# A two-layer block with attention and a mixture of experts: the first expert's last rows are listed on chip, roots for two blocks at once, shorter groups of products

## The chip, the cores and the metric

The kernel runs on one core of one Trainium2 chip. TensorE (PE) multiplies matrices out of on-chip memory (SBUF) into eight accumulation banks (PSUM); VectorE (DVE), ScalarE (ACT) and GpSimd (POOL) work on rows of 128 partitions; SyncE (SP) issues DMA transfers, and GpSimd issues the indirect ones, which gather or scatter rows by a list of row numbers. Each engine runs its own instructions strictly in order and waits on semaphores for the others. The metric is device time in microseconds, lower is better.

## The reference

```
h  = x + attention(layernorm(x))          # 2048 tokens x 512, 32 heads of 16, window 256, causal
g  = softmax(layernorm(h) @ wg)           # 8 experts; the two best, their weights scaled to sum 1
out = h + sum over the 2 experts of  w * (gelu(layernorm(h) @ w1[e]) @ w2[e])    # w1: 512x1376, w2: 1376x512
```

All is float32. The kernel writes each large product as three products of rounded halves: high x high, high x low, low x high.

## The kernel before

**Stages.** The tokens go through in four chunks of 512 (`NC` = 4). For each chunk come layernorm and the projections, attention by groups of four heads, and `project(c)`: output projection, residual, second layernorm, gate, and the choice of two experts (`route`). After that `experts()` goes through the eight experts, one after the other. Expert 0 comes first always; the other seven come by size, for which `rank_experts` sorts the counts (`run`) and SyncE reads the order (`pick_expert`).

**The table.** For each choice of a token, `route` computes a slot number: expert times `SLOTS` plus the place among that expert's tokens. On GpSimd, `scatter` writes the token's row number and its weight (8 bytes) into that slot of `table` in DRAM. An expert's rows are then found by `fetch` (SyncE: a piece of the table into `tb_t`), `turn_x` (GpSimd: an indirect gather of 128 rows of the normalized tokens `xnd` into `xg_t`; TensorE: four transposes; ScalarE and VectorE: the high and low halves), `up` (w1, then gelu), `down` (w2), a scaling by the weight, and an indirect scatter-add into the output.

**The first expert's two parts.** Expert 0 holds 598 slots: five tiles of 128 columns, the last of 86. Its first 384 slots (`EARLY`) are filled by chunks 0 to 2, so their fetch, their gathers and their up-projections (384 columns) run beside the last chunk's projection and routing. For that, the last chunk's counts for expert 0 are raised to 384 at least. The other two tiles (214 columns) need the last chunk: its last scatter, then a second fetch (`f1`), then two gathers.

**The last chunk** (`end`) is routed in two halves of two blocks of 128 tokens: for each half `s1` (two largest gates, VectorE), `s3` (TensorE: places by a triangular 0/1 matrix), `s2`, `s2b` (weights), `s4` (slots), then four scatters. `rstd` computes the inverse root of the variance on GpSimd, for one block at a time here, and the normalized block goes to `xnd` by DMA and through a transpose (`turn`) to the gate's product.

**What sets the order.** Every piece of work is a task with an engine, an estimated duration, a priority and buffers. `Plan.order` runs through all tasks in estimated time and writes out one fixed order; an engine takes the ready task of the lowest priority. Dependencies given to `plan.after` or in a task's list shape only this order; on the chip an instruction waits for the data that it uses. Two raw-weight buffers (`m_raw`), two temporaries and seven PSUM banks (`one`) are handed out in that order too.

The prediction's steps touch: L1316 and L1321 (gather and transposes of `turn_x`), L1348 (`up`), L1380 (`down`), L1243 (`fetch`), L1102 (scatter), L1209 (load of w1), L480 (low halves on GpSimd), L476 (high halves on ScalarE), L998 and L1005 (transposes and products of the gate), L1266 (small products for the later experts), L1092 to L1098 (`s4`), and L1134 (the first step of the sort).

## Time and profile before

| | us |
|---|---|
| runs shown | 1045.19, 1047.86, 1051.26 |
| median | 1047.86 |
| profiled execution: its own time | 1044.5 |
| profiled execution: span of the trace | 1042.4 |

The profile is of one execution. Its times count from the first instruction. Busy shares of the span are 98% for TensorE, 62% for VectorE, 52% for ScalarE and 60% for GpSimd. The last chunk's projection and routing, with expert 0's early part among them, lie between some 480 and 550 us, and the experts fill the time from there to the end. In a timeline, each row gives the start, the duration from the first start to the last end of the merged instructions, the engine, the line, what is written and read with its shape, and the count; in square brackets the idle time before it and what ended it. A float32 product shows as two instructions. Rows of the granted clock give TensorE's clock as a share of 2.4 GHz.

### The profile page before, as it was taken

The numbers are of one execution on the slowest core, as the hardware profiler recorded it, in microseconds if no ns is written. First come the engines' busy times: TensorE is split into PE (matmuls) and PEld (weight loads), VectorE is DVE, ScalarE is ACT, GpSimd is POOL, SyncE is SP. The second block draws the span as 40 slices with busy tenths as digits, with TensorE's granted clock in tenths as the row PEclk, the third lists the DMA queues.
The fourth block names the chain that finished last, engine by engine and source line by source line (L and its number), as shares of the span: only waits on it lengthen the run. The fifth ranks groups of instructions, "written<-read, shape, count | busy, mean of one in ns | idle before, by whom it ended". The sixth has DMA issues, their size and how long they took to land. (4 is left out here: it accounts for less than half of the span.)

```text
span 1042.4 us, 19919 instructions
## 1 busy us (share of the span) xinstructions
PE 1016.8 (98%) x6722; PEld 842.0 (81%) x6722; DVE 645.6 (62%) x1951; ACT 536.9 (52%) x1143; POOL 623.3 (60%) x986
## 2 busy tenths in 40 slices
PE   8999999999999999998898999999999999999997
PEld 5877777877777777754887898998999989878795
DVE  8888876887677777787752556345453554544440
ACT  3487747575766656577631555163462543525340
POOL 5687749777887958758495144186483763834111
PEclk9999999999999999999998999999999999999999
DMA  6999877768696978764516344264444544454522
GB/s 214 291 249 240 250 190 214 224 179 202 191 251 164 200 159 210 201 167 110 190 49 148 97 141 113 63 153 111 115 97 128 157 94 105 123 139 151 124 77 29
DMA packets 143887, 164.48 MB, mean 158 GB/s; under 512 B 68587, under 2 KB 86571, under 8 KB 143776
## 3 DMA queue, kind: packets, MB, share of 16 engines
q1 hardware_dynamic: 128448, 145.96, 50.3%
q0 software_dynamic: 15328, 17.16, 9.9%
q8 instruction: 55, 0.90, 0.4%
q14 instruction: 56, 0.46, 0.2%
HBM read 111.10 MB, written 51.43 MB: 156 GB/s over the span
## 5 line engine op out<-in xcount | busy, mean ns | idle before, releaser
L735 DVE CUSTOM_DVE_ANT_0 one<-one,masked 128x320 f32<-128x320 f32 (+4 forms) x512 | 230.3, 494 | 57.9 <-PE one L730 55.0
L1348 PE MATMUL one<-mr 128*128 128x288 f32 (+14 forms) x1716 | 255.9, 310 | 1.3 <-ACT mr L476 0.7
L1348 PEld LDWEIGHTS one<-mr 128*128 128x128 f32 (+1 forms) x1716 | 244.5, 187 | 10.1 <-ACT mr L476 0.9
L785 ACT ACTIVATE zone<-one 128x384 f32<-128x384 f32 (+1 forms) x480 | 208.6, 495 | 80.1 <-PE one L779 60.6
L811 POOL TENSOR_SCALAR_AFFINE_SELECT zone<-zone 128x256 f32<-128x256 f32 (+1 forms) x332 | 151.1, 479 | 61.2 <-ACT zone L785 59.4
L1380 PE MATMUL one<-zone,mr 128*128 128x512 f32 (+4 forms) x648 | 154.9, 394 | 0.0
L480 POOL TENSOR_TENSOR mr<-mf,mr 128x512 fp32r<-128x512 f32 (+4 forms) x99 | 123.8, 1262 | 41.7 <-ACT mr L476 39.9
L1380 PEld LDWEIGHTS one<-zone,mr 128*128 128x128 f32 (+4 forms) x648 | 117.0, 182 | 31.4
L779 PE MATMUL one<-mr 98*128 98x384 f32 (+1 forms) x592 | 138.5, 327 | 3.1 <-ACT zone L785 1.9
L476 ACT CAST mr<-mf 128x512 fp32r<-128x512 f32 (+6 forms) x152 | 108.3, 734 | 46.0 <-DMA mf<-in_A_wqk_dram 15.3
L779 PEld LDWEIGHTS one<-mr 98*128 98x128 f32 x592 | 96.0, 190 | 42.9 <-ACT zone L785 14.1
L730 PE MATMUL one<-mr 96*128 96x320 f32 (+4 forms) x512 | 122.8, 315 | 1.5 <-DVE mx L735 0.9
L1287 POOL DMA_INDIRECT mf<-xnd,mf x94 | 106.4, 1132 | 28.8 <-issue 26.9
L1403 POOL DMA_INDIRECT out_dram<-mf,tb x24 | 41.5, 1730 | 130.6 <-DVE mf L1391 116.4
L478 DVE TENSOR_TENSOR mr<-one,mr 128x512 fp32r<-128x512 f32 (+16 forms) x161 | 79.1, 509 | 58.3 <-ACT mr L476 58.0
L1362 ACT ACTIVATE one<-one 128x288 f32<-128x288 f32 (+13 forms) x132 | 54.7, 415 | 104.1 <-PE one L1348 103.2
L661 PE MATMUL one<-mr 128*128 128x512 f32 (+1 forms) x396 | 103.7, 389 | 3.0 <-ACT mr L476 2.8
L730 PEld LDWEIGHTS one<-mr 96*128 96x128 f32 x512 | 87.7, 190 | 22.2 <-DVE mx L735 11.6
L1403 POOL DMA_INDIRECT out_dram<-mf x40 | 65.9, 1648 | 65.6 <-DVE mf L1433 57.1
L835 PE MATMUL oT<-zone 128*17 128x384 f32 (+2 forms) x1408 | 95.7, 389 | 0.1
L476 ACT CAST mr<-one 128x512 fp32r<-128x512 f32 (+16 forms) x161 | 70.6, 448 | 31.5 <-PE one L1321 17.3
L476 ACT CAST zone<-mf 128x512 fp32r<-128x512 f32 x72 | 42.1, 620 | 78.0 <-PE one L1423 48.5
(189 smaller groups left out, 1282.9 us busy)
## 6 DMA issues: line engine op xcount, KB each, us to landing
mf<-in_B_w_dram SPq DMA_DIRECT2D x32, 688.0 KB
mf<-in_B_w_dram SPq DMA_DIRECT2D x40, 512.0 KB
qkd<-mr SPq DMA_DIRECT2D x29, 512.0 KB
mr<-qkd SPq DMA_DIRECT2D x128, 96.0 KB
mr<-qkd SPq DMA_DIRECT2D x32, 384.0 KB
mf<-in_A_x_dram SPq DMA_DIRECT2D x32, 256.0 KB
mf<-in_A_wqk_dram SPq DMA_DIRECT2D x32, 256.0 KB
qkd<-mr SPq DMA_DIRECT2D x64, 128.0 KB
```

The lines of the kernel that those rows point to most:

```text
L476: a = add("ACT", 51 + n * 0.86, lambda: nc.scalar.copy(dst_h(), src()), deps, prio, bufs)
L480: b = add("POOL", 60 + n * 2.3, lambda: nc.gpsimd.tensor_sub(dst_l(), src(), f32(dst_h())), [a], prio, bufs)
L661: nc.tensor.matmul(single[bk.h][:, s], wt()[:, int(i == 1), k * 128:(k + 1) * 128], xt[:, k, s], start=(i == 0 and k == 0), stop=(i == 2 a ...
L730: nc.tensor.matmul(view()[:, j], q_of(slot)[0:96, h + j, b].rearrange("p e q -> p (e q)"), K[slot.h][0:96, h + j, (b + k0) * 64:(b + 5) * ...
L735: nc.vector.tensor_tensor_reduce(v, v, masked[:, 320 - n:], scale=1.0, scalar=NEG, op0=OP.add, op1=OP.max, accum_out=mx_t[slot.h][:, h + j ...
L779: nc.tensor.matmul(single[bk.h][:, off:off + w], K[slot.h][0:98, h // 2, r * 128:(r + 1) * 128], q_of(slot)[0:98, h // 2, 2 * b:2 * b + 2 ...
L785: return add("ACT", 51 + n * 0.833, lambda: nc.scalar.activation(dst(), single[bk.h][:, 0:n].rearrange(order, **({"e": 2, "q": 64} if "e" ...
L811: nc.gpsimd.affine_select(v, v, pattern=[[0, v.shape[1]], [-1 if far else 1, 128]], compare_op=OP.is_gt if far else OP.is_ge, fill=0.0, ba ...
L1287: nc.gpsimd.indirect_dma_start(out=xg_t[i][:, t * 128:(t + 1) * 128], out_offset=None, in_=xnd4, in_offset=bass.IndirectOffsetOnAxis(ap=ql ...
L1348: nc.tensor.matmul(bank(), a[:, k, f * 128:f * 128 + w], spot[b][:, k, c0:c1], start=(i == 0), stop=(i == 11))
L1380: nc.tensor.matmul(single[bk.h][:n], h[a][:w], spot["w2"][2 * f + b][:w], start=(f == 0 and q == 0), stop=(f == NF - 1 and q == 2))
L1403: d = nc.gpsimd.indirect_dma_start(in_offset=None, compute_op=OP.add, **kw)
```

## The change

**On-chip list.** Expert 0's piece of the table is fetched once, all five tiles, before any scatter of the last chunk (`plan.after` holds those back behind the fetch). What the last chunk adds is then found by products: `numbers` puts the slot numbers 385 to 640 into a row (`late_no`), `find` compares it with each token's slot in expert 0 (`late_v`) and so gets a 0/1 matrix of 128 tokens by 256 slots for each block, and `pick_late` multiplies that matrix with two columns, token number and weight (`late_r`), summed over the four blocks in one bank. `merge` takes the larger of the fetched and the picked token number, adds the weights, and writes both into `tb_t`. The two late gathers follow from that. The scatters of the last chunk stay, since the overflow path of expert 0 and the other experts read the table.

**Roots** for two blocks at once in the last chunk (`rstd` with n = 2), with the two blocks' normalizations after them; two buffers for the transposed block (`nt_2`).

**Shorter groups.** Expert 0's `up` is three tasks of four products, its `down` one task for each 128 rows of w2. Expert 0's low halves of w2 all go to VectorE.

The sort now stands after `merge`. The core of the diff (`...` marks what is left out):

```diff
-                f0 = fetch(0, b + -12, sum((route_done[c] for c in range(NC - 1)), []) + [xn_done[i] for i in range(4 * NC - 4)], 0, EARLY // 128)
-                f1 = fetch(0, b - 8, all_routes + all_xn, EARLY // 128, nt)
+                f0 = fetch(0, F0_PRIO, sum((route_done[c] for c in range(NC - 1)), []) + [xn_done[i] for i in range(4 * NC - 4)], 0, nt)
+                for t in route_done[NC - 1]:
+                    plan.after(t, [f0])
+                tb0 = tb_t[0][:, EARLY // 128:nt]
+                old = add("DVE", 100, lambda: nc.vector.tensor_copy(late_t, tb0[:, :, 0]), [f0] + hot[:1], b - 10)
+                def merge():
+                    ps = single[hot[1].h][:, 0:4].rearrange("p (i q) -> p i q", q=2)
+                    nc.vector.tensor_tensor(late_t, late_t, ps[:, :, 0], op=OP.max)
+                    nc.vector.tensor_copy(tb0[:, :, 0], late_t)
+                    nc.vector.tensor_add(tb0.bitcast(F32)[:, :, 1], tb0.bitcast(F32)[:, :, 1], ps[:, :, 1])
+                f1 = add("DVE", 550, merge, [old] + hot[2:], 36, [hot[1]])
+                xg_use[2] = p2_free + hot[2:]
+                plan.after(sort, [f1])
...
+            def numbers():
+                nc.gpsimd.iota(late_no.bitcast(I32), pattern=[[1, 256]], base=EARLY + 1, channel_multiplier=0)
+            def number_rows():
+                nc.vector.tensor_copy(late_no, late_no.bitcast(I32))
+                nc.vector.tensor_copy(late_r[:, :, 0], tok[:, 4 * c:4 * c + 4])
...
+                for i in range(2):
+                    Vv.tensor_mul((late_r[:, b0:b0 + nb, 1], late_w[:, 0:nb])[i], oh[:, i, :, 0], w[:, i, :, 1])
+                Vv.tensor_add(late_r[:, b0:b0 + nb, 1], late_r[:, b0:b0 + nb, 1], late_w[:, 0:nb])
...
+        def find():
+            pos = single[bk.h][:, 0:nb * E].rearrange("p (b e) -> p b e", e=E)
+            Vv.tensor_add(t["u"], pos, over(e_pos))
+            Vv.scalar_tensor_tensor(late_v[:, b0:b0 + nb], t["u"][:, :, 0], 1.0, t["m"][:, :, 0], op0=OP.add, op1=OP.mult)
+            for b in range(nb):
+                Vv.tensor_scalar(late_p[b], late_no, late_v[:, b0 + b:b0 + b + 1], None, op0=OP.is_equal)
+        def pick_late():
+            ps = single[hot[1].h][:, 0:4].rearrange("p (i q) -> p i q", q=2)
+            for b in range(nb):
+                for i in range(2):
+                    nc.tensor.matmul(ps[:, i], late_p[b][:, i * 128:(i + 1) * 128], late_r[:, b0 + b], start=(b0 + b + i == 0), stop=(b0 + b == 3),
...
+                    root = rstd(lambda b0=b0: mv_t[0][:, b0:b0 + 2, 1], lambda b0=b0: ry_t[0][:, b0:b0 + 2], seen[-2:], pb + 0.4, 2)
...
-                                 src, dd, lo="POOL" if e == 0 and f >= 3 else "DVE"))
+                                 src, dd))
...
-            for f0, f1 in ((0, 4), (4, 8), (8, 10), (10, NF)):
+            for f0, f1 in [(f, f + 1) for f in range(NF)] if e == 0 else ((0, 4), (4, 8), (8, 10), (10, NF)):
...
-                fx[i] = (turn_32 if e in BY32 else turn_x)(e, i, f0 if i < EARLY // 128 else f1, b + (-12 + 3.8 if e == 0 and i < EARLY // 128 else -5.2) + 0.8 * i, up_last[e - 1] if e else [])
+                fx[i] = (turn_32 if e in BY32 else turn_x)(e, i, f0 if i < EARLY // 128 else f1, 36.0 + 0.1 * i if e == 0 and i >= EARLY // 128 else b + (X0 if e == 0 else -5.2) + 0.8 * i, up_last[e - 1] if e else [])
```

Up to the third transpose of the early tiles, TensorE's order is word for word the old one, and so is that of the other engines up to about there, but for the size of the first fetch (five tiles for three). From the last tile of expert 0's `down` on, TensorE's order is the old one again. Between them it moves. In the rows below, line numbers of the changed kernel are its own: its L1424 is `up` (L1348 before), L1455 `down` (L1380), L1385 the transposes of gathered rows (L1321), L1156 `pick_late`, L1380 the gather (L1316), L1161 the scatter (L1102), L486 the low halves (L480). `one` is a PSUM bank, `zone` and `mr` hold weights and halves, `mf` float32 data.

TensorE, expert 0's late tiles, before:

```order
L1380 MATMUL one_77<-zone_5885,mr 128x512 x12
L1266 MATMUL one_74<-rm,pick 128x20 x2
L1321 MATMUL one_76<-ident,mf 128x128 x4
L1380 MATMUL one_77<-zone_5885,mr 128x512 x3
L1380 MATMUL one_77<-mr 128x512 x3
L1321 MATMUL one_75<-ident,mf 128x86 x4
L1321 MATMUL one_78<-ident,mf 128x128 x4
L1380 MATMUL one_77<-mr 128x512 x3
L1321 MATMUL one_80<-ident,mf 128x128 x4
L1348 MATMUL one_79<-mr 128x214 x12
```

and now:

```order
L1424 MATMUL one_74<-mr 96x384 x4
L1455 MATMUL one_75<-zone_5885,mr 128x512 x9
L1156 MATMUL one_76<-mf 128x2 x4
L1455 MATMUL one_75<-zone_5885,mr 128x512 x18
L1455 MATMUL one_75<-mr 128x512 x6
L1385 MATMUL one_77<-ident,mf 128x128 x4
L1455 MATMUL one_78<-zone_5885,mr 128x512 x3
L1385 MATMUL one_79<-ident,mf 128x86 x4
L1455 MATMUL one_78<-zone_5885,mr 128x512 x9
L1424 MATMUL one_74<-mr 128x214 x12
```

The late tiles' transposes stood behind three tiles of `down`; they now stand behind one tile and the second pick, and the late up-projections follow after 12 products of the second tile.

GpSimd, from the last of the last chunk's eight scatters to the late gathers, before:

```order
L1101 MEMSET spacer 1x1
L1102 DMA table<-ent_6257,si_6290 18432x2
L480 TENSOR_TENSOR mr<-mf,mr 128x384 x2
L480 TENSOR_TENSOR mr<-mf,mr 96x384
L1316 DMA mf<-xnd,tb_147 128x512
L1316 DMA mf<-xnd,tb_147 86x512
```

and now, from the fourth of the eight:

```order
L1161 DMA table<-ent_6134,si_6197 18432x2
L1130 COPY ent_6255<-tok 128x2 x2
L486 TENSOR_TENSOR mr<-mf,mr 128x384 x2
L486 TENSOR_TENSOR mr<-mf,mr 96x384
L1380 DMA mf<-xnd,tb_147 128x512
L1380 DMA mf<-xnd,tb_147 86x512
L1160 MEMSET spacer 1x1
L1161 DMA table<-ent_6255,si_6295 18432x2
```

The two gathers stood behind all eight scatters; they now stand between the first half's four and the second half's four, with three low halves of the up-projections ahead of them.

VectorE, the second half's routing, before:

```order
L1082 TENSOR_TENSOR e_pos<-e_row,run 128x8
L1084 TENSOR_SCALAR ent_6257<-oT 128x2 x2
L1092 TENSOR_TENSOR oT<-one_74,e_pos 128x16
L1093 TENSOR_TENSOR run<-run,one_74 128x8
L1094 TENSOR_TENSOR r_oh<-r_oh,oT 128x32
L1096 TENSOR_REDUCE oT<-r_oh 128x4
L1098 CAST si_6290<-oT 128x4
L1134 TENSOR_SCALAR mf<-run 1x8
```

and now:

```order
L1123 TENSOR_SCALAR ent_6255<-oT 128x2 x2
L1127 TENSOR_TENSOR mf<-r_oh,ent_6255 128x2 x2
L1128 TENSOR_TENSOR mf<-mf 128x2
L1147 TENSOR_TENSOR oT<-one_80,e_pos 128x16
L1148 SCALAR_TENSOR_TENSOR mf<-oT,r_m 128x2
L1150 TENSOR_SCALAR mf<-mf 128x256 x2
L1138 TENSOR_TENSOR run<-run,one_80 128x8
L1139 TENSOR_TENSOR r_oh<-r_oh,oT 128x32
L1141 TENSOR_REDUCE oT<-r_oh 128x4
L1143 CAST si_6295<-oT 128x4
L1536 TENSOR_TENSOR mf<-mf,one_76 128x2
L1537 CAST tb_147<-mf 128x2
```

The weights' product, the slot's value, the two comparisons (L1150) and the merge (from L1536 on) now stand ahead of the sort. On SyncE the two loads of the next expert's first weights stood behind the register loads for all seven experts and two fetches; they now stand behind the register loads for two experts, ahead of the fetches.

## Rows read from the trace of the kernel before

**Rows 1.** The page: the span, and busy time, share of the span and instructions of TensorE and its weight loads with the other engines.

```profile
span 1042.4 us, 19919 instructions
...
PE 1016.8 (98%) x6722; PEld 842.0 (81%) x6722; DVE 645.6 (62%) x1951; ACT 536.9 (52%) x1143; POOL 623.3 (60%) x986
```

**Rows 2.** Waits of TensorE over the whole span: who waited, for whom, us in total, times, the longest.

```profile
PE one L1321 <- DMA mf<-xnd,tb: 6.0, 3, 2.8
...
PE one L1321 <- DVE mf L905: 2.1, 1, 2.1
...
PE one L1348 <- DVE mr L478: 0.6, 1, 0.6
```

**Rows 3.** Timeline of TensorE, from the early tiles to the first products of expert 1: start, us, engine, line, operation, out<-in, count, idle time before and what ended it.

```profile
494.80 0.72 PE L1321 MATMUL one<-ident,mf 128*128 128x128 f32 x4 [1.90 <-DMA mf<-xnd,tb]
...
519.47 0.95 PE L1005 MATMUL one<-wgt,mf 128*128 128x8 f32 x8
520.28 1.07 PE L998 MATMUL one<-ident,mf 128*128 128x128 f32 x8
...
553.25 2.94 PE L1380 MATMUL one<-zone,mr 128*128 128x512 f32 x12
556.02 0.52 PE L1266 MATMUL one<-rm,pick 128*128 128x20 f32 x4
557.88 0.75 PE L1321 MATMUL one<-ident,mf 128*128 128x128 f32 x4 [1.34 <-DMA mf<-xnd,tb]
...
562.81 1.76 PE L1321 MATMUL one<-ident,mf 86*128 86x86 f32 x8 [2.79 <-DMA mf<-xnd,tb]
564.23 1.63 PE L1380 MATMUL one<-mr 96*128 96x512 f32 x3
565.65 1.05 PE L1321 MATMUL one<-ident,mf 128*128 128x128 f32 x4
566.36 16.11 PE L1348 MATMUL one<-mr 128*128 128x214 f32 x132
582.30 1.57 PE L1321 MATMUL one<-ident,mf 128*128 128x128 f32 x12
...
599.46 19.29 PE L1348 MATMUL one<-mr 128*128 128x288 f32 x144
```

**Rows 4.** Stretches of two us: busy time of each engine (instructions), then the granted clock of TensorE, the share of the DMA engines and GB/s.

```profile
560.00:562.00 2.00, 0.02 (x1) 0.00 (x0) 0.00 (x0) 0.00 (x0) 1.66 (x3) 1.00 0.94 141
...
566.00:568.00 2.00, 2.00 (x12) 2.00 (x11) 0.70 (x1) 0.00 (x0) 1.01 (x1) 0.50 0.28 75
...
570.00:572.00 2.00, 2.00 (x20) 2.00 (x20) 0.73 (x2) 0.75 (x3) 0.00 (x0) 1.00 0.55 97
```

**Rows 5.** Timeline of GpSimd: the early gather and low halves of w1, the first and last step of the four root chains, low halves, the last two scatters, the late gathers.

```profile
491.31 1.00 POOL L1316 DMA_INDIRECT mf<-xnd,tb  x1 [1.49 <-DMA tb<-table]
...
493.60 3.23 POOL L480 TENSOR_TENSOR mr<-mf,mr 128x688 fp32r<-128x688 f32 x2
...
512.73 0.24 POOL L487 TENSOR_SCALAR mvh<-mvh 128x1 f32<-128x1 f32 x1
...
520.49 0.19 POOL L495 TENSOR_TENSOR ryh<-ryh,mvh 128x1 f32<-128x1 f32 x1
...
538.50 1.99 POOL L480 TENSOR_TENSOR mr<-mf,mr 128x384 fp32r<-128x384 f32 x2
...
543.27 0.96 POOL L1102 DMA_INDIRECT table<-ent,si  x1 [0.22 <-issue]
...
544.53 0.96 POOL L1102 DMA_INDIRECT table<-ent,si  x1 [0.22 <-issue]
...
551.33 0.99 POOL L1316 DMA_INDIRECT mf<-xnd,tb  x1 [2.64 <-DMA tb<-table]
```

**Rows 6.** Timeline of SyncE's DMA queue: the fetches of the table and the first weights of the next expert.

```profile
548.78 1.04 SPq L1243 DMA_DIRECT2D tb<-table  x2
...
551.04 0.98 SPq L1209 DMA_DIRECT2D mf<-in_B_w_dram  x2
```

**Rows 7.** Timeline of ScalarE: four high halves of w2, and two of the late up-projections' activations.

```profile
509.09 2.18 ACT L476 CAST zone<-mf 128x512 fp32r<-128x512 f32 x4
...
571.92 0.33 ACT L1362 ACTIVATE one<-one 128x214 f32<-128x214 f32 x1 [0.64 <-PE one L1348]
...
573.26 0.33 ACT L1362 ACTIVATE one<-one 128x214 f32<-128x214 f32 x1 [0.64 <-PE one L1348]
```

**Rows 8.** Timeline of VectorE: the products with the inverse sums, and steps of the second half's routing and of the sort.

```profile
493.29 4.30 DVE L905 TENSOR_TENSOR mf<-mf 128x128 f32<-128x128 f32 x4 [1.80 <-DMA mf<-od]
...
531.42 0.16 DVE L1098 CAST si<-oT 128x4 int32<-128x4 f32 x1
...
534.17 0.17 DVE L1058 TENSOR_TENSOR r_m<-oT,r_oh 128x16 bf16<-128x16 f32 x1
...
534.46 0.15 DVE L1082 TENSOR_TENSOR e_pos<-e_row,run 128x8 f32<-128x8 f32 x1
...
534.77 0.23 DVE L1084 TENSOR_SCALAR ent<-oT 128x2 f32<-128x2 f32 x2 [0.16 <-ACT oT L1112]
...
538.67 1.86 DVE L1134 TENSOR_SCALAR mf<-run 1x8 f32<-1x8 f32 x1
```

91 lines of the change are left out of this document (71 added, 20 removed).

## The prediction

> **What bounds the kernel now.** Read the page first. The span is 1042.4 us and TensorE is busy for 1016.8 of it, 98% [rows 1]. Nothing that leaves TensorE's own work alone can bring more than about 25 us, and the list of its waits says where those lie: 6.0 us are three waits of the transposes of gathered rows (L1321) for the gather of those rows out of xnd, and 2.1 more are put down to DVE at the same line [rows 2]. The timeline splits them. Two of the three waits, 1.34 us and 2.79 us, stand at 557.9 and 562.8 us, where expert 0's two late tiles are turned [rows 3]. The third, 1.90 us, stands at 494.8 us before the early tiles [rows 3]; TensorE, VectorE and GpSimd do the same things in the same order there, before and after, so I count nothing for it. Then read the granted clock: after the wait at 560 it stands at 0.50, the lower level of 1.2 GHz, until about 569 us, and is back at 1.00 in 570 to 572 [rows 4]. From there to the end TensorE waits once, 0.63 us at 619 [rows 2]. So the change can win at one place: between 556 and 570 us.
>
> Why do those transposes wait? The chain is on GpSimd and SyncE. The last routing scatter into the table goes out at 544.5 [rows 5], the table comes back only after it has landed, at 548.8 [rows 6], the gather starts at 551.3, and 256 KB of rows then share the DMA engines with two weight loads of 688 KB that SyncE issues at 551.0 [rows 5, 6]. The rows are there at 557.9, 6.5 us after their gather was issued. At the early tiles the same gather took 3.5 us from issue to the transpose (491.31 to 494.80) [rows 3, 5].
>
> **What goes.** The two waits are 1.34 + 2.79 = 4.1 us. The slow clock costs more, worked out from TensorE's starts [rows 3]: 8 transposes take 1.42 us (562.81 to 564.23), but 4 take 0.36 at full clock by 0.71 / 2, so 0.7 are lost; 3 products of 512 columns take 1.42, and 12 take 2.77 at 553.25, so 0.7; 4 transposes take 0.71, so 0.4; the 11 late up-projections take 15.94 us (566.36 to 582.30), and at full clock their activations follow each other every 1.34 us [rows 7], which is 14.7, so 1.2. Together 3.0 us. What goes is 7.1 us, if nothing is late in their place.
>
> **What comes onto TensorE.** Each half of the last chunk's routing gets four products of two columns (pick_late). The nearest row above is the gate: four products of 8 columns against 128x128 weights take 0.81 us, 519.47 to 520.28 [rows 3]. The nearest below is the pair of products of 20 columns (L1266), at most 0.52 us a pair [rows 3], so four of two columns are hardly under 0.4. I take the gate's 0.81, the same shape but for columns: 2 x 0.81 = 1.6 us, bounds 0.8 to 2.1. They lie on the bound engine and cost all of it. Shorter groups of products (three of four for twelve, one block of w2 at a time) add no product, and TensorE changes weights at every product anyway: nothing. Splitting the low halves of w2 and roots for two blocks at once: four root chains stand in a row on GpSimd from 512.7 to 520.7 [rows 5], and two chains of two blocks halve that. Neither is on TensorE, whose early up-projections cover it. It costs nothing as long as that cover lasts, to about 536 us; what it buys is that gates and routing come earlier.
>
> **Is the list in time?** Count from the moment at which the first half's slots are written (si). In the trace that CAST stands at 531.42, and the second half's chain runs to m at 534.3 and to the weights' write at 535.0 [rows 8], 3.4 us behind si. In the changed order one split of 96x512 comes in (about 0.65), then five small steps of 0.15 to 0.2, then the two comparisons that make the 0/1 matrix (128x256 each). I put 0.3 on each, between 0.15 (the smallest DVE row) and 0.5 (a 128x512 split is 0.7). So the matrix is ready about 5.5 us behind si. Adding up the changed order by these rows, si falls near 532 us, so the matrix is there near 538, and TensorE reaches the second pick near 538.3: after the eleven early up-projections, the first pick and nine products of tile 0. It fits, just.
>
> Then the merge, 0.5 us plus two hops: 540 to 541. GpSimd has meanwhile sent the first half's four scatters (1.25 each [rows 5]) and made the last three low halves (0.99 each), and is free at about 540.7. Gathers start near 541.2 and 542.5, land 3.5 us later by [rows 3, 5], so at 544.7 and 546. TensorE, after the pick and 24 products of 0.23, wants them near 544.7 and 545.8. SyncE's loads of the next expert's weights follow the sort (2 us) and two register loads, near 545, behind the gathers and not with them. In place of the two waits I expect 0 to 1.5 us, and take 0.8.
>
> **New small waits**, each bounded by what it would wait for: the last block's projection behind one copy and four w2 casts on ScalarE (2.18 for four [rows 7]), 0 to 1.0, take 0.4; the first pick behind a comparison that waits for one low half on GpSimd, 0 to 1.0, take 0.3; a gate behind a copy on ScalarE, 0.2. With the gathers, 1.7 us.
>
> **The sum**, against the profiled execution (1044.5 us, span 1042.4): -4.1 - 3.0 + 1.6 + 1.7 = -3.8 us, so 1040.7. That execution lies 3.4 us under the median of the runs shown, 1047.86; against the median the forecast is 1044.0 us, -0.37%.
>
> **A rule that speaks against it.** The comparisons read and write SBUF on VectorE while GpSimd makes low halves. The trace shows what that does: L1134, one row of 8 numbers, took 1.86 us while GpSimd ran two L480 from 538.50, and a like step at 534.46 took 0.15 [rows 5, 8]; the four L905 at 493.29 took 4.30 us while GpSimd ran 3.23 us of L480 [rows 5, 8]. The Trainium skill, "SBUF — State Buffer", section "SBUF: two separate sides", says that VectorE (in a two-port mode, or with two SBUF inputs) and GpSimd share a port pair under an exclusive lock: who starts first holds it for the whole instruction, and the other fully blocks. The trace agrees, and shows that GpSimd's next instruction may keep it. If the comparisons come first, that rule costs nothing here; if GpSimd's three low halves do, it is the second rival.
>
> **Rivals.** (1) *All hidden.* None of the new waits bites, and the wait at 619 us goes as well, since the next expert's weights have more time. -7.1 - 0.6 + 1.6 + 0.3 = -5.8: 1042.1 us. For it: all my margins are near zero, not clearly negative. Against: so many in a row.
> (2) *The shared port, and the slower side.* The second half's comparisons meet GpSimd's copies and three low halves, which by [rows 5] start 5.2 to 5.6 us behind si, while the comparisons start at 5.0 and end at 5.5. If GpSimd is first, they wait for three of 0.99 us; TensorE stands 3 us before the second pick, and such a wait is what ended in the lower clock at 562 us [rows 3, 4], another 3.0. The gathers then find TensorE late and cost nothing. -7.1 + 1.6 + 0.9 + 3.0 + 3.0 = +1.4: 1049.3 us. It decides from a wait of more than about 2.3 us at that pick with the clock lost, and from 4.6 without. Held up for one low half alone it is 1.0 to the bad, inside the forecast's range.
> (3) *The gathers are late all the same*, since the next weights' loads meet them: 6.5 us from issue to use as now, not 3.5. The second tile then stands 3 us instead of 0.8. -3.8 + 2.2 = -1.6, and 1.7 more if half of that clock loss comes back: 1046.3 to 1048.0 us. The change would not do what it says. For it: the trace shows that price once; against: the loads need the sorted order first, which comes after the merge.
>
> **How the numbers follow.** The forecast has 0.47, all hidden 0.23, the shared port 0.15, late gathers 0.15. A measurement of this kernel tells some 0.5%, 5.2 us, from no change. All hidden is over it for the most part (0.20), the forecast in its upper end (0.08): faster 0.28. The shared port passes +5.2 us only if the first pick meets it as well: slower 0.06. Same 0.66. The range: below, all hidden with the picks at their lower bound, 1041.0; above, the shared port, 1049.8, since the unknown waits can add up.
>
> **What would show it.** Right: no wait over 1 us at the transposes of expert 0's last tiles, granted clock 1.00 from 510 us on, pick rows of about 0.1 us each, the first products of expert 1 (599.5 us before [rows 3]) at about 595.7. Late gathers: a wait for xnd at the second of those transposes. Shared port: a comparison of over 1 us on DVE, and TensorE idle before the second pick. Wrong altogether: a time outside the range with TensorE unchanged between 500 and 600 us, or a new wait behind expert 1, where the order is the old one.

## The result and the profile after

| | us | runs |
|---|---|---|
| before, median (lowest to highest) | 1047.72 (1042.26 to 1052.63) | 20 |
| after, median (lowest to highest) | 1053.06 (1049.23 to 1057.16) | 20 |
| after / before | 1.0057, 95% interval 1.0044 to 1.0070 | |

By the ratio the change makes the kernel about 6.0 us slower (the two medians lie 5.3 us apart), where 3.8 us faster was forecast. The profiled execution after took 1052.77 us.

The page after, span and TensorE's busy time [rows 1]:

```profile
span 1051.0 us, 19953 instructions
...
PE 1022.1 (97%) x6738; PEld 844.7 (80%) x6738; DVE 654.4 (62%) x1977; ACT 536.4 (51%) x1143; POOL 609.4 (58%) x971
```

TensorE is busy 5.3 us longer, and the rest of the 8.6 us by which the spans differ is idle time. Waits of TensorE after [rows 2]; the lines are now L1385 (transposes of gathered rows), L1029 (transposes for the gate), L1156 (picks):

```profile
PE one L1385 <- DMA mf<-xnd,tb: 6.8, 3, 5.0
...
PE one L1029 <- DVE mf L1009: 0.9, 1, 0.9
...
PE one L1156 <- DVE mf L1150: 0.5, 1, 0.5
```

Timeline of TensorE after [rows 3], from the first early up-projection (L1424) to the first product of expert 1 (L1414); L1455 is `down`:

```profile
506.46 4.44 PE L1424 MATMUL one<-mr 128*128 128x384 f32 x24 [0.68 <-ACT mr L482]
...
519.53 1.28 PE L1029 MATMUL one<-ident,mf 128*128 128x128 f32 x8 [0.94 <-DVE mf L1009]
...
543.58 0.61 PE L1156 MATMUL one<-mf 128*128 128x2 f32 x4 [0.49 <-DVE mf L1150]
...
549.72 0.63 PE L1385 MATMUL one<-ident,mf 128*128 128x128 f32 x4
550.11 0.94 PE L1455 MATMUL one<-zone,mr 128*128 128x512 f32 x3
556.01 0.85 PE L1385 MATMUL one<-ident,mf 86*128 86x86 f32 x4 [4.96 <-DMA mf<-xnd,tb]
...
607.52 17.77 PE L1414 MATMUL one<-mr 128*128 128x288 f32 x132
```

The first late tile (128 rows) is no longer waited for. The second (86 rows) is, for 4.96 us instead of 2.79. Stretches of two us after [rows 4]: the lower clock follows that wait as it did before.

```profile
558.00:560.00 2.00, 2.00 (x6) 1.60 (x5) 0.00 (x0) 0.00 (x0) 0.00 (x0) 0.50 0.86 97
564.00:566.00 2.00, 2.00 (x20) 2.00 (x19) 0.46 (x2) 1.00 (x3) 1.39 (x3) 1.00 0.66 211
```

GpSimd after [rows 5]: three low halves (L486), then the two late gathers (L1380). SyncE after [rows 6]: the next expert's first two loads of w1. VectorE after [rows 8]: the comparisons of the first and of the second half (L1150).

```profile
541.40 1.97 POOL L486 TENSOR_TENSOR mr<-mf,mr 128x384 fp32r<-128x384 f32 x2
543.55 1.00 POOL L486 TENSOR_TENSOR mr<-mf,mr 96x384 fp32r<-96x384 f32 x1 [0.18 <-ACT mr L482]
545.36 1.01 POOL L1380 DMA_INDIRECT mf<-xnd,tb  x1 [0.81 <-DVE mf L1201]
546.68 1.46 POOL L1380 DMA_INDIRECT mf<-xnd,tb  x1 [0.30 <-issue]
```

```profile
548.25 0.98 SPq L1273 DMA_DIRECT2D mf<-in_B_w_dram  x2
```

```profile
533.09 1.05 DVE L1150 TENSOR_SCALAR mf<-mf 128x256 f32<-128x256 f32 x2
...
540.57 2.96 DVE L1150 TENSOR_SCALAR mf<-mf 128x256 f32<-128x256 f32 x2
```

The gather of 128 rows was issued at 545.36 and used 4.4 us later without a wait. The gather of 86 rows was issued at 546.68 and used 9.3 us later, with two weight loads issued 1.6 us behind it. And the second half's comparisons took 2.96 us against 1.05.

**Where the time went**, by four places in the two timelines:

| | before | after | difference |
|---|---|---|---|
| to the first early up-projection | 503.63 | 506.46 | +2.83 |
| from there to expert 1 (changed stretch) | 95.83 | 101.06 | +5.23 |
| expert 1 to the last product of the kernel | 436.24 | 435.41 | -0.83 |
| last product to the end of the span | 6.71 | 8.12 | +1.41 |

The first row is not the change's: the order is the same there, the lower clock near 460 us lasts 3.4 us in the one execution and 10.2 in the other, and in all seventeen profiles of this study that first up-projection lies between 502.9 and 511.1 us, without regard to the variant (0 to 17 us of lower clock near 460). The other three rows make 5.8 us, about the 6.0 measured. In the changed stretch TensorE waits 6.39 us in place of 4.13 (waits over 0.15 us), both executions spend the same 6.83 us at the lower clock, and TensorE's own work (the stretch without its waits) grows by 3.0 us, from 91.7 to 94.7, 1.78 of it the picks. The clock costs both about the same: in the runs below that keep the full clock in this stretch, own work is 88.9 to 89.1 us in the order of before and 91.6 to 92.2 in the order of the change, 2.5 to 3.0 us less.

### The profile page after: what moved, and what is told of

Read it like the earlier page. It is cut to its first block, busy times and chain, and to the rows that moved or that the text cites. A ratio compares the mean times of both kernels' runs of the same rounds, so it can differ in the third digit from the quotient of the medians.

```text
span 1051.0 us, 19953 instructions
## 1 busy us (share of the span) xinstructions
PE 1022.1 (97%) x6738; PEld 844.7 (80%) x6738; DVE 654.4 (62%) x1977; ACT 536.4 (51%) x1143; POOL 609.4 (58%) x971
## 5 line engine op out<-in xcount | busy, mean ns | idle before, releaser
L1414 PE MATMUL one<-mr 128*128 128x290 f32 (+15 forms) x1452 | 214.5, 309 | 0.0
L1414 PEld LDWEIGHTS one<-mr 128*128 128x128 f32 (+1 forms) x1452 | 205.8, 186 | 8.0
L1455 PE MATMUL one<-zone,mr 128*128 128x512 f32 (+4 forms) x648 | 158.1, 398 | 0.0
L486 POOL TENSOR_TENSOR mr<-mf,mr 128x512 fp32r<-128x512 f32 (+4 forms) x97 | 121.9, 1265 | 49.9 <-ACT mr L482 49.1
L1455 PEld LDWEIGHTS one<-zone,mr 128*128 128x128 f32 (+4 forms) x648 | 117.9, 184 | 31.5 <-DVE mr L484 0.2
L482 ACT CAST mr<-mf 128x512 fp32r<-128x512 f32 (+5 forms) x152 | 108.5, 733 | 42.1 <-DMA mf<-in_A_wqk_dram 14.0
L667 PEld LDWEIGHTS one<-mr 128*128 128x128 f32 x396 | 69.2, 189 | 16.0 <-ACT mr L482 5.5
```

The source lines that it names most:

```text
L482: a = add("ACT", 51 + n * 0.86, lambda: nc.scalar.copy(dst_h(), src()), deps, prio, bufs)
L486: b = add("POOL", 60 + n * 2.3, lambda: nc.gpsimd.tensor_sub(dst_l(), src(), f32(dst_h())), [a], prio, bufs)
L667: nc.tensor.matmul(single[bk.h][:, s], wt()[:, int(i == 1), k * 128:(k + 1) * 128], xt[:, k, s], start=(i == 0 and k == 0), stop=(i == 2 a ...
L1414: nc.tensor.matmul(bank(), a[:, k, f * 128:f * 128 + w], spot[b][:, k, c0:c1], start=(i == 0), stop=(i == 11))
L1455: nc.tensor.matmul(single[bk.h][:n], h[a][:w], spot["w2"][2 * f + b][:w], start=(f == 0 and q == 0), stop=(f == NF - 1 and q == 2))
```

## The experiments

All times below are ratios to the kernel before in the same series, so the changed kernel stands at 1.0057. "Stretch" is the time from the first early up-projection to expert 1: 95.83 before, 101.06 after.

### Weights held behind the gathers, and the comparison in another form

`hold`: SyncE copies one word of each gathered tile, which makes it wait for the landing, before it loads w1 of expert 1.

```diff
+            if e == 1 and w == 1 and not held_w:
+                for n, t in enumerate(late_rows):
+                    held_w.append(add("SP", 60, lambda n=n: nc.sync.dma_start(landed[:, n:n + 1], xg_t[EARLY // 128 + n][0:1, 0:1]), [t] + held_w, prio - 0.01))
-            l = dma(ld, ..., picked.get(e, []) + (late_rows if e == 1 and w == 1 else []) + hold, ...)
+            l = dma(ld, ..., picked.get(e, []) + (held_w if e == 1 and w == 1 else []) + hold, ...)
```

> The changed kernel, with expert 1's four w1 loads held on SP until both late gathers have landed (SP copies one word of each gathered tile ahead of the loads); TensorE, VectorE, ScalarE and GpSimd orders are unchanged. Theory A (the loads, issued at 548.25 right behind the sort, share the DMA engines with the second late gather): the wait of 4.96 us before the second late transpose falls to under 1 us, the half clock of 6.8 us behind it goes too (3.4 us), and the time falls from 1053.1 to about 1045 (ratio to the kernel before about 0.997). Rival B (the gather is slow by itself, by its 1.46 us of descriptors on GpSimd or by the four scatters right behind it in the same queue): the wait stays over 4 us and the time at 1053 (1.0055). Rival C (some other load is late next: expert 1's weights): the wait goes, but a new one of 2 us or more appears at the first products of expert 1.

Measured: 1.0038 (1.0022 to 1.0054), stretch 97.49. TensorE, and GpSimd's gathers, in this run:

```profile
546.22 0.63 PE L1389 MATMUL one<-ident,mf 128*128 128x128 f32 x4
546.61 0.94 PE L1459 MATMUL one<-zone,mr 128*128 128x512 f32 x3
550.09 0.71 PE L1389 MATMUL one<-ident,mf 86*128 86x86 f32 x4 [2.54 <-DMA mf<-xnd,tb]
```

```profile
541.84 1.01 POOL L1384 DMA_INDIRECT mf<-xnd,tb  x1 [0.82 <-DVE mf L1202]
543.16 1.46 POOL L1384 DMA_INDIRECT mf<-xnd,tb  x1 [0.30 <-issue]
```

The loads cost half of the wait, and 2.54 us stay with nothing but small scatters beside the gather. So theory A is not the whole cause. The packets of the two gathers, each packet two rows (the last of each train of the second gather has one), tell why:

```
gather of 128 rows: 64 packets, starts from 543.56 to 544.62 us
gather of  86 rows: 44 packets, starts from 545.35 to 549.57 us, among them
   547.69 547.85 548.00 548.17 548.33 548.48 548.64 548.79 548.95 549.10 549.26
   547.70 547.86 548.01 548.17 548.33 548.48 548.64 548.79 548.95 549.10 549.26
```

The second gather is two trains, side by side, of one packet every 0.155 us: it looks like two DMA engines of sixteen. (In the changed kernel the same packets start between 548.88 and 555.22.) From here on this is theory D.

`port` writes the comparison as a product of two tensors in form; `both` has the two edits together:

```diff
-                Vv.tensor_scalar(late_p[b], late_no, late_v[:, b0 + b:b0 + b + 1], None, op0=OP.is_equal)
+                Vv.tensor_tensor(late_p[b], late_no, late_v[:, b0 + b:b0 + b + 1].to_broadcast([128, 256]), op=OP.is_equal)
```

> The changed kernel, with the 0/1 comparison written as VectorE's tensor_tensor against a broadcast column in place of tensor_scalar with a column operand; all orders are unchanged. Theory P (the second half's two comparisons took 2.96 us, against 1.05 us in the first half, because VectorE's form of that operation on SBUF data waits for the three GpSimd subtractions beside it): both halves take 0.7 to 1.2 us, the merge and the late gathers come about 2 us earlier, the wait of 0.49 us at the second pick goes; the weight loads, which stand behind the sort, come 2 us earlier too, so they still meet the second gather, whose wait stays at 3 to 4.5 us: about 1051 to 1052.5 (ratio 1.0035 to 1.005). Rival: the comparisons were late for another reason (their operands, a semaphore) and still take about 3 us beside GpSimd's subtractions; nothing moves, 1053 (1.0055).

> Both edits together: weights of expert 1 held until the late gathers land, and comparisons as tensor_tensor. Theories A and P together: no wait over 1 us between the first up product of expert 0 and the first of expert 1, full clock there, about 1044 (ratio 0.9965), half a us to one us under the hold alone. Rival B: 1051 or more. If this is at or over the hold alone, the delay of 2 us by the comparisons was hidden anyway.

Measured: port 1.0073 (1.0048 to 1.0097), both 1.0018 (1.0000 to 1.0035). The second half's comparisons in the port run, and its late transpose:

```profile
539.74 0.76 DVE L1150 TENSOR_TENSOR mf<-mf 128x256 f32<-128x256 f32 x2
```

```profile
554.63 0.85 PE L1385 MATMUL one<-ident,mf 86*128 86x86 f32 x4 [5.04 <-DMA mf<-xnd,tb]
```

The comparisons fall from 2.96 to 0.76 us as expected, the wait at the pick goes, and no gain shows in the time. The gain stops at TensorE's own order: the pick stands behind nine products of tile 0, and the merge on VectorE now waits 1.66 us for the pick. The stretch is 99.42 us in this run, 1.6 less than in the changed kernel, of which 0.49 is the wait at the pick; in `both` it is 96.47, 1.0 less than with the hold alone, and the times of `both` and `hold` can't be told apart. So the delayed comparisons were all but hidden: theory P's delay is there, and worth nothing that a time shows.

`before_hold` is the same hold in the kernel before.

> The kernel before, with expert 1's w1 loads held on SP in the same way until both late gathers have landed; expert 1's table fetch, which stands behind them on SP, waits too. Theory A, if it holds for the kernel before as well (its loads were issued at 551.04 and its late gathers at 551.33 and 552.62): the waits of 1.34 and 2.79 us at the late transposes fall by 2.5 us or more in sum, the half clock from 562 to 569 goes (3.4 us): about 1042 (ratio 0.9945). Rival B: no change or slower, by up to 2 us as expert 1's rows come later (1.000 to 1.002).

Measured: 0.9954 (0.9935 to 0.9973), stretch 89.39. There the waits at the late transposes fall from 4.13 to 0.45 us and the clock stays at 1.00 behind them:

```profile
558.76 0.70 PE L1325 MATMUL one<-ident,mf 128*128 128x128 f32 x4
...
561.30 1.23 PE L1325 MATMUL one<-ident,mf 86*128 86x86 f32 x8 [0.45 <-DMA mf<-xnd,tb]
```

```profile
562.00:564.00 2.00, 2.00 (x17) 1.86 (x16) 0.52 (x1) 0.45 (x1) 1.15 (x3) 1.00 0.88 146
```

One dependence, without the list, takes away all but 0.45 us of the two waits that the list was to remove, and the lower clock with them. It could do so with 86 rows because TensorE comes to the second tile late there: 6.8 us after that gather's issue (554.07 us) in this run, and 7.4 us in the kernel before. The changed order brings TensorE there 4.4 us after the issue, in the changed kernel as in `hold`, and the two trains took 6.4 us without the weights.

### How many rows a gather takes

The changed kernel with n = 96, 89 or 88 rows in place of 86 in its second late gather; the extra rows are loaded and not used.

```diff
-                nc.gpsimd.indirect_dma_start(out=xg_t[j][:w], ..., in_offset=bass.IndirectOffsetOnAxis(ap=tb_t[e][:w, i, 0:1], axis=0))
+                n = 96 if e == 0 and w == 86 else w
+                nc.gpsimd.indirect_dma_start(out=xg_t[j][:n], ..., in_offset=bass.IndirectOffsetOnAxis(ap=tb_t[e][:n, i, 0:1], axis=0))
```

> The changed kernel, with the second late gather taking 96 rows instead of 86 (the ten extra rows are loaded and never used); every order and every other instruction is unchanged, and the weight loads come as in the changed kernel. Theory D, formed from the packets of the held run: the gather of 86 rows dribbles, one packet of two rows every 0.08 us from 546.1 to 550.1 with no weights beside it, as if two of the sixteen DMA engines carried it, while the gather of 128 rows before it moved 64 such packets in 1.2 us; 96 rows should be spread over all engines. Then the gather lands within 4 us of its issue, the wait of 4.96 us falls to under 0.5 us although the weight loads stand where they stood, the half clock behind it goes: about 8 us less, 1045 on the chip of the first result (ratio 0.997 to 0.999). Theory A alone (weights collide, the row count is nothing): the wait stays at 4.5 us or more and the ratio at 1.0057.

> The changed kernel with 89 rows in the second late gather (three extra rows, loaded and not used). Theory D in the words of the Trainium skill (DMA: Bandwidth & Descriptors, Why a DMA increments its semaphore by 16 and not by 1: the number of engines is the largest one up to 16 that divides the row count; 100 rows go on 10, 127 on 1): 89 is a prime, so one engine carries 45 packets; at 0.155 us each, the spacing within one train of packets in the held run, that is 7.0 us with nothing beside them and more beside the weights: the wait before the second transpose grows from 4.96 to over 8 us. A theory by which only the bytes count: unchanged, 5 us.

> The same with 88 rows, one row less than the run beside it. By the same rule eleven engines carry 44 packets, four each: 0.6 us of packets, and the wait before the second transpose falls from 4.96 us to under 0.7 us, as with 96 rows. If the rule is that the count must be a multiple of 16: as with 86 or 89 rows, a wait of 5 us or more.

Measured: with 96 rows 0.9994 (0.9975 to 1.0012) and a stretch of 93.55. With 89 rows one run of 1058.55 us and with 88 one of 1042.67, where the kernel before had a median of 1045.57 and went from 1040.36 to 1049.15; for these two the profile of the one run speaks, not the time. The second late transpose with 96, with 89 and with 88 rows, one fence each:

```profile
553.58 0.71 PE L1386 MATMUL one<-ident,mf 86*128 86x86 f32 x4 [0.21 <-DMA mf<-xnd,tb]
```

```profile
561.92 0.85 PE L1386 MATMUL one<-ident,mf 86*128 86x86 f32 x4 [10.86 <-DMA mf<-xnd,tb]
```

```profile
548.44 0.60 PE L1386 MATMUL one<-ident,mf 86*128 86x86 f32 x4
```

```
rows   packets   first to last packet start     wait of TensorE
 86      44         548.88 to 555.22                4.96
 96      48         550.74 to 552.65                0.21
 89      45         from 551.12, one train         10.86
 88      44         545.93 to 547.16                none
```

One row less, 88 for 89, takes 10.86 us off a wait. Bytes don't explain that; the divisors do. The Trainium skill, "DMA: Bandwidth & Descriptors", section "Why a DMA increments its semaphore by 16 and not by 1", says that a DMA goes on the largest number of engines up to 16 that divides the slowest dimension of both its sides, which here is the row count. That makes 2 engines for 86, 16 for 96, 1 for 89 and 11 for 88, and the four rows above agree with it. A rule of multiples of 8 does not fit as well: eight shares of 11 rows would each leave a packet of one row, and all 44 packets of the 88 rows have two.

The price stood in GpSimd's own rows too, in the trace of before as well. Issuing the gather took 0.99 us with 128 rows, 0.94 with 96, 1.01 with 88, 1.46 with 86 and 2.08 with 89. Before (86 rows), and with 89:

```profile
552.62 1.46 POOL L1316 DMA_INDIRECT mf<-xnd,tb  x1 [0.30 <-issue]
```

```profile
546.68 2.08 POOL L1381 DMA_INDIRECT mf<-xnd,tb  x1 [0.30 <-issue]
```

With 96 rows the weights were loaded where the changed kernel loads them, and the half clock was gone, so theory A as I first put it falls: the loads lengthened a gather that was slow already.

`rows96_port`, `before_rows96` and `list_off96` put the same 96 rows into three other kernels: the changed one with the other comparison, the kernel before, and the changed one with the late slots read from the table in DRAM again (roots, groups and low halves as changed). The core of the last:

```diff
-                f0 = fetch(0, F0_PRIO, ..., 0, nt)
...
-                f1 = add("DVE", 550, merge, [old] + hot[2:], 36, [hot[1]])
+                f0 = fetch(0, b + -12, ..., 0, EARLY // 128)
+                f1 = fetch(0, b - 8, all_routes + all_xn, EARLY // 128, nt)
...
-            a2 = add("DVE", 1100, find, [b_, a2] + hot[2:], p, [bk])
-            hot.append(add("PE", 500, pick_late, [a2], p, [hot[1]]))
```

> 96 rows and the comparisons as tensor_tensor, weights not held. Theories D and P: no wait over 1 us between the first up product of expert 0 and the first of expert 1, no half clock there; the both run measured 1.0018 with a wait of 2.55 us and 3.4 us of half clock left in it, so 1.0018 less 4.2 us of 1046: about 0.998. If theory D is wrong: 1.005.

> The kernel before, with 96 rows in its second late gather and nothing else. Its late gathers were followed by waits of 1.34 and 2.79 us and by 6.8 us of half clock. Theory D: the 2.79 goes and the half clock with it, 5 to 6 us less, ratio about 0.995, as the hold of the weights gave for this kernel (0.9954) by another way. Theory A: the wait stays, ratio 1.000.

> The changed kernel without the list: the late slots come through the table in DRAM as before; roots for two blocks, shorter groups and the low halves of w2 on VectorE stay; 96 rows in the second late gather. It parts the change in two: against the kernel before with 96 rows it is what roots and groups cost, against the changed kernel with 96 rows and the port edit it is what the list brings. If roots and groups cost nothing (my prediction took 0.2 us for them): equal to before_rows96 within 0.1 per cent, about 0.995. If the paired roots cost the wait of 0.95 us at the second gate transposes and the shorter groups some tenths: 0.996 to 0.997. If the list is what costs: this is faster than the changed kernel with 96 rows and the port edit by 2 us or more.

Measured: 1.0015 (0.9994 to 1.0036), 0.9980 (0.9961 to 1.0000), 1.0035 (1.0014 to 1.0055). All three miss what was expected (0.998, 0.995, and 0.997 or less). The port edit again brings nothing. In the kernel before, 96 rows shorten the stretch less than the hold does (90.99 us against 89.39; the two times can't be told apart): there the loads are issued ahead of the gathers, and the first gather, of 128 rows, was late for them. SyncE's loads, GpSimd's gather and TensorE in that run:

```profile
553.92 1.03 SPq L1209 DMA_DIRECT2D mf<-in_B_w_dram  x2
```

```profile
554.24 0.99 POOL L1317 DMA_INDIRECT mf<-xnd,tb  x1 [2.17 <-DMA tb<-table]
```

```profile
562.14 0.75 PE L1322 MATMUL one<-ident,mf 128*128 128x128 f32 x4 [2.00 <-DMA mf<-xnd,tb]
```

So the collision is real where 1.4 MB of weights stand ahead of the gather, 7.9 us from issue to use, and costs 0.21 us where they are issued 1.6 us behind it (rows96). The run without the list has the highest ratio of the three, though it can't be told from rows96_port: roots, groups and low halves alone wait 0.96 us at the gate's transposes (for the norms behind the paired roots), 3.2 at the late gathers and 0.84 in `up`, and its end is 1.4 us longer (below).

### The other parts

`groups_off96`: 96 rows, and expert 0's groups as long as before.

```diff
-                if e:
+                if 1:
                     d = add("PE", 12 * max(107, mm_ns(n) + 2.5), mm, deps, prio, [pb] + lim)
-            for f0, f1 in [(f, f + 1) for f in range(NF)] if e == 0 else ((0, 4), (4, 8), (8, 10), (10, NF)):
+            for f0, f1 in ((0, 4), (4, 8), (8, 10), (10, NF)):
```

> The changed kernel with 96 rows in the second late gather, and with the groups of products of expert 0 as long as before (12 products of an up block in one piece; a down tile in four pieces). In the 96-row run TensorE's own work between the first up product and expert 1 took 91.9 us outside of waits against 88.9 to 89.0 in the kernel before with hold or with 96 rows: 1.8 of it the picks, some 1.2 the rest, with 49 changes from one kind of product to another in place of 34. Theory G (a change of kind costs about 0.09 us; shorter groups make 10 to 15 more of them): own work 90.7 to 91.2, and if no wait grows, 1 us less in all, ratio 0.998 to 0.999. Rival: the gates and sorts, which then stand behind longer groups, come later by up to 0.7 us each and a wait takes it back: 0.9995 to 1.001.

Measured: 0.9988 (0.9969 to 1.0007), which can't be told from 0.9994. In the trace TensorE's work falls into 32 pieces of one kind of product each instead of 49, its own work is 91.6 us instead of 91.9, and its waits are 0.8 us instead of 1.7. The shorter groups bought no time, and cost at most a few tenths; theory G's size was too large. The wait of 0.94 us at the gate's transposes is gone in this run, though the paired roots are in it.

`before_hold_rows96` has both mends in the kernel before.

> The kernel before with both mends of its late gathers: the w1 loads of expert 1 held until they have landed, and 96 rows in the second. With the hold alone a wait of 0.45 us was left at the late transposes, none with half clock behind it. Expected: that wait goes and nothing else moves, ratio 0.9945 to 0.9955, the fastest of all. If the loads, which start earlier than with the hold alone, do something else, it shows as a wait at expert 1.

Measured: 0.9935 (0.9914 to 0.9957), by the ratio 6.8 us under the kernel before. It is the lowest ratio of the study, but can't be told from the hold alone (0.9954, 0.9935 to 0.9973). No wait is left at the late transposes. Something else did move: two other waits show in its profile, 1.30 us at 570 and 1.66 us at 617; before_hold has nothing at the first place, and 0.16 and 0.57 us in expert 1.

`after_pad` adds three dummy instructions to GpSimd's queue at the start; `list_alone96` has the list without paired roots and short groups, with 96 rows and the dummies (the low halves of w2 stay on VectorE as changed); `mended` has list and paired roots, groups as long as before, 96 rows, the hold and the dummies.

```diff
         nc.gpsimd.tensor_copy(spacer, f32(xl)[0:1, 3, 511:512])
+        for _ in range(3):
+            nc.gpsimd.memset(spacer, 0.0)
```

The root for each block, in the list-alone kernel:

```diff
-                if b % 2:
-                    b0 = b - 1
-                    root = rstd(lambda b0=b0: mv_t[0][:, b0:b0 + 2, 1], lambda b0=b0: ry_t[0][:, b0:b0 + 2], seen[-2:], pb + 0.4, 2)
-                    for b1 in (b - 1, b):
+                if 1:
+                    root = rstd(lambda b=b: mv_t[0][:, b, 1:2], lambda b=b: ry_t[0][:, b:b + 1], seen[-1:], pb + 0.4, 1)
+                    for b1 in (b,):
```

> The changed kernel with three dummy GpSimd memsets of one word at the start of the program, where GpSimd is idle. Theory T: from TensorE's last product to the end of the span it is 8.1 to 8.5 us in every kernel whose GpSimd queue holds up to 1147 records and 6.5 to 6.7 us in every kernel with 1148 or more, because GpSimd stands still for its last page of instructions only in the former; the list took GpSimd's four subtractions and others away and so moved the page's edge. Then three more instructions bring the tail from 8.1 to 6.6 us, and the time falls by 1.4 to 1.5 us: ratio 1.004 to 1.0045 against 1.0057, the wait of 4.96 us unchanged. Rival: the tail follows what the kernel does before it (loads, stores), and stays at 8.1 us: 1.0057.

> The list alone: the changed kernel with a root for each block and groups of products as long as before, 96 rows in the second late gather, and the three dummy memsets. Against the kernel before with 96 rows it shows what the list brings and costs. From the runs so far: 1.8 us of picks on TensorE, the waits of 2.0 (late gathers) and 2.2 us (expert 1's rows) gone, so 2 to 2.5 us less than before_rows96 (0.998): 0.9955 to 0.996, if nothing new waits. If the list only pays with roots for two blocks and short groups: new waits of 1 us or more at the picks or gates, and 0.998 or more.

> The changed kernel with list and roots for two blocks, groups as long as before, 96 rows in the second late gather, expert 1's w1 loads held until it has landed, and the three dummy memsets: the best that the runs so far make of the change. From groups_off96 (0.9988, tail 8.3 us) less 1.6 us of tail: about 0.997; the hold should add nothing, since with 96 rows the gather was not waited for any more. If the held loads matter beyond the gather, 0.995 or less, level with the kernel before with the same two mends (0.9935).

Measured: 1.0048 (1.0031 to 1.0065), 1.0001 (0.9984 to 1.0018), 1.0005 (0.9987 to 1.0024). The last products of the changed kernel, whose span is 1051.0, and of the padded one, whose span is 1052.6:

```profile
1041.38 1.55 PE L1455 MATMUL one<-mr 128*70 128x512 f32 x6
```

```profile
1044.58 1.55 PE L1457 MATMUL one<-mr 128*70 128x512 f32 x6
```

From the last product to the end it is 8.1 us in the one and 6.5 in the other. All seventeen profiles fall on the same two sides: 8.1 to 8.5 us in the eight kernels with 1146 or 1147 records of GpSimd, 6.5 to 6.7 in the nine with 1148 or more (records of its sequencer included, which the page leaves out). The traces show where the time goes: in each of the eight, GpSimd stands still ahead of its 1141st record, 1.5 to 2.1 us beyond the moment at which all that it waits for is there (1050.24 us in the changed kernel, where the last signal came at 1048.61). In `list_off96`, whose program is one record shorter, that is one instruction later in the ending, ahead of the same 1141st record. The nine show no such stall. So 1.4 us of the change's loss hang on where in GpSimd's program its end falls. That a page of instructions is loaded late at that place is argued, not shown. The time moved by 0.9 in a thousand, inside the interval. `hold` and `both` have 1148 records: 1.4 us of what they gain over the changed kernel in the profiles lie here, and not at the gathers.

The list alone and the mended change both come out level with the kernel before: my expectations of 0.996 and 0.997 were wrong. The mended change is slower than the kernel before with the same two mends (0.9935); the list alone can't be told from the kernel before with 96 rows (0.9980). In the mended run the stretch is 94.65 us: the late transposes wait no more, but `up` waits 0.81 us at 558 for the halves of the gathered rows, and 2.32 at 625 for a low half on VectorE. TensorE there, and VectorE just before that:

```profile
625.17 15.07 PE L1421 MATMUL one<-mr 128*128 128x288 f32 x111 [2.32 <-DVE mr L487]
```

```profile
623.68 1.10 DVE L1366 STREAM_TRANSPOSE mf<-mf 128x512 f32<-128x512 f32 x1 [6.25 <-DMA mf<-xnd,mf]
624.70 1.14 DVE L487 TENSOR_TENSOR mr<-one,mr 128x290 fp32r<-128x290 f32 x3
```

VectorE stood 6.25 us for the gather of expert 2's rows, and the low halves for which TensorE waited were queued behind it.

The hold is the likely cause in this run. `groups_off96` has the same order on TensorE, VectorE, ScalarE and GpSimd (but for the three dummies), and only lacks the hold and the dummies. SyncE's w1 loads in `groups_off96` and in the mended run:

```profile
548.09 1.07 SPq L1273 DMA_DIRECT2D mf<-in_B_w_dram  x2
```

```profile
557.50 1.05 SPq L1279 DMA_DIRECT2D mf<-in_B_w_dram  x2
```

Counted from the first early up-projection (506.52 and 508.84 us), the loads go out 41.6 us behind it without the hold and 48.7 with it, and the next experts' fetches of the table stand behind them. Without the hold the two waits are not there, the stretch is 92.41 us instead of 94.65, and from expert 1 to the last product it is 435.30 instead of 437.93. So in the changed order the mend that helped the kernel before goes with 4.9 us more in the profile, where I had expected it to add nothing; the two times, 0.9988 and 1.0005, can't be told apart. Such waits come without a hold too: the list-alone run has 0.92 us at 522.8 and 1.94 at 624 for low halves on VectorE and 0.77 at 558.8, the kernel before with 96 rows 2.19, and the kernel before itself 0.63 [rows 2]; the changed kernel has none behind expert 1. With the late gathers mended, no run shows that the list saves time, and its picks cost 1.6 to 1.9 us.

## Why the prediction was wrong

The sum of the prediction beside what the profiles measured, in us:

| term | forecast | measured |
|---|---|---|
| waits at the two late transposes (1.34 + 2.79) | -4.1 + 0.8 | 4.96 in their place: +0.8 |
| lower clock behind them | -3.0 | as long in both, 6.83 us at the lower level: 0 |
| eight picks | +1.6 | +1.78 |
| other new waits | +0.9 | 0.94 + 0.49 = +1.4 |
| other work of TensorE, shorter groups among it | 0 | +1.2 |
| behind expert 1 | 0 | -0.8 |
| last product to the end | 0 | +1.4 |
| sum | -3.8 | +5.8 |

**The step that failed** is "Gathers start near 541.2 and 542.5, land 3.5 us later by [rows 3, 5], so at 544.7 and 546." The 3.5 us were the price of a gather of 128 rows, and I put them on one of 86. The 86 rows went in two trains, as on two DMA engines: 6.4 us from issue to the start of the last packet without weights beside them (hold), 8.5 with them. The rest of the step came near: less the 2.8 us by which this execution was late from the start, the gathers were issued 1.3 us later than forecast, and TensorE came to the second tile (551.05) 2.4 us later. The first gather kept the 3.5 us well enough to cause no wait, so the method was right and the shape was not. The trace of before held the clue: the 2.79 us stood at the 86-row tile [rows 3], its gather took 1.46 us to issue where that of 128 rows took 0.99, and I laid the whole delay on the weights. The same slip ended the clock term, since a wait of 4.96 us brings the lower clock back as one of 2.79 did.

**Right in the mechanism:** the two waits that bounded the stretch, and that the weights collide with the first gather (before_hold); the 128-row tile lost its wait; the picks' price, 1.78 for 1.6; and what the lower clock costs, 2.5 to 3.0 us for the 3.0 of the sum. **The third rival** (late gathers) is the case that came, at a larger price than its 1046.3 to 1048.0, and the reason that it gave, the loads, holds for half of the wait only. **The second rival's** mechanism came too: comparisons of 2.96 us beside GpSimd's low halves. But TensorE waited 0.49 us for them, not 3, and undoing it brought nothing that a time shows.

**The roots** did not come free, as the prediction had it: the pairs' norms come later together, and TensorE waits 0.94 us for the first of them at 518.6. It does so with the short groups only; with groups as long as before (groups_off96) the paired roots cause no wait there. The 1.2 us of other work I can't put to one part: groups_off96 gives back 0.3, but the list alone, without roots and groups, has 1.2 us over the kernel before as well (92.1 less 1.9 of picks, against 89.0 with the same 96 rows).

**Still open:** whether GpSimd's stall at the end is a load of instructions; what the other work of 1.2 us is; and why, in one series, the changed order with 96 rows (groups_off96, 0.9988) stays 5 in a thousand over the kernel before with both mends (0.9935). Their profiles differ by 2.0 us in the stretch, -1.9 behind it and 1.8 at the end, together 1.8 us, where the medians differ by 4.6.

## What to carry to other kernels

Before a transfer's time is taken from one row for another, compare the row counts, not only the bytes: an indirect gather of 86 rows was slower than one of 128, and ten unused rows took the wait away. A wait at a transfer can be mended at the transfer (who is issued ahead of it, how it is spread) before a chain of work is rebuilt to start it earlier; here one dependence gave 0.9954 and, with ten rows more, 0.9935 (not to be told apart), and the rebuilt chain 1.0057. A mend holds for the order in which it was tried: in the changed order the same hold went with later weights and new waits (mended). And a chain that lets an engine come earlier also leaves less time to the transfer that it comes to, here 4.4 us in place of 7.4. Last, a wait that is taken off one engine is worth only what the engine's next place in order lets through, as the comparisons showed.

## What the runs showed of the hardware

- One row decides over 10 us: the second late gather was waited for 10.86 us with 89 rows and not at all with 88, with the same kernel around it. The count shows in GpSimd's time for the issue too: 0.94 to 1.01 us for 88, 96 and 128 rows, 1.46 for 86, 2.08 for 89. One train of two-row packets (4 KB) moves one packet every 0.155 us without other traffic.
- The end of the program, from the last product on, was 8.1 to 8.5 us or 6.5 to 6.7 us by a few GpSimd instructions more or less: three dummies at the program's start brought it from 8.1 to 6.5. In all eight of the longer ends GpSimd stood still 1.5 to 2.1 us ahead of the same place in its program, its 1141st record, with nothing left to wait for.
- The second of the two late comparisons took 2.63 to 2.73 us in all nine kernels that wrote it as tensor_scalar, and 0.42 in all three that wrote it as tensor_tensor. In each it starts while GpSimd writes a scatter's descriptors, and in the nine it ends with GpSimd's second low half, which comes behind that. The Trainium skill, "SBUF — State Buffer", section "SBUF: two separate sides", has the exclusive lock that I cited in the prediction; by it the one that starts first goes on. Against the low halves alone the traces differ: the second comparison started 0.5 to 0.6 us before the first low half, where the one of the first half took 0.33 to 0.35 us, and was held all the same. GpSimd was writing descriptors before the comparison began; if that counts as the one that started first the rule would hold, but the comparison just ahead ran inside the same writing in 0.35 to 0.42 us. No run settles this. In the three kernels the low halves started after the comparison had ended, so that form and moment are not wholly told apart.
